# Moving the second group's loads, the last group's layer-norm statistics and the last projection steps in a one-core attention and gMLP block

## The chip, the cores and the metric

The kernel runs on one core of a Trainium2 chip. The core has five engines that run side by side and wait for each other on semaphores: TensorE (PE in the profile, with its weight loads as PEld), VectorE (DVE), ScalarE (ACT), GpSimd (POOL) and SyncE (SP), which here issues nearly all transfers. The metric is the device time of one execution in microseconds (us), taken as the median of several runs. A profiled execution is one further run; its span goes from the first to the last instruction.

## What is computed

One transformer block with adaptive layer norm: attention with a key and value cache, then a gMLP. Sizes: 2048 tokens of width 512, 32 query heads that share 8 key and value heads, head width 128, 2048 keys; in the MLP 896 columns in each half.

```python
sa, ca, ga, sb, cb, gb = split(silu(c) @ w_mod)          # six rows of 512
h = layernorm(x) * (1 + ca) + sa
x = x + ga * A(h)                                        # attention
h = layernorm(x) * (1 + cb) + sb
x = x + gb * B(h)                                        # gMLP

def A(x):
    q = (x @ wq).reshape(2048, 32, 128)                  # 4 query heads per kv head
    p = softmax(q @ k.T * 128 ** -0.5)
    return (p @ v).reshape(2048, 4096) @ wo

def B(x):
    z = gelu(x @ w_in)
    z1, z2 = z[:, :896], layernorm(z[:, 896:])
    g = w_sp @ z2 + b_sp[:, None]                        # w_sp is 2048 x 2048, over tokens
    return (z1 * g) @ w_out
```

## The kernel before

**Units and slots.** Attention is cut into 128 units: 8 groups g (one key and value head each, with its four query heads) of 16 units, one for each tile j of 128 tokens. Unit u belongs to group u // 16 and tile u % 16. Every unit is emitted in 8 slots. A slot of unit u has, in this order: what was put on a list for it (`at(unit, slot, function)`, L993), the two score products of unit u (`qk`, L1011 or L1030, into an `s_ps` bank pair) with the exponential that ACT takes of them (L1018 or L1037), the next share of the PV products of an earlier unit (`pv` L1086, `pv_rows` L1065, into an `o_ps` bank), a piece of a query projection for a later block (`fill`, L947, into a `misc` bank, copied out by DVE at L958), and in some slots one product of the output projection of a still earlier unit (`wo_proj`, L1143, into a `misc` bank). There are two `misc` banks, two `o_ps` banks and two pairs for `s_ps`. Each engine carries out its instructions in the order in which they are emitted; nothing reorders them.

**Units by rows.** From unit 8 up to 118 two of three units keep their probabilities by query rows, and four DMA transposes on SP for each such unit (L1050) turn them into the layout that PV needs. The other units compute the scores already turned and need none. The PV products of a unit run one to three units later, and the output projection two or three units after these. In units by rows each head has its own projection product, and DVE multiplies it by 1/sum while it adds it to `xacc` (L1136); in the others four products accumulate in one bank and DVE adds once (L1130). The output of a unit that is not by rows is turned by a DMA transpose (`oT`, L1109); in these units DVE takes a reciprocal (L1097) and a normalising multiply (L1098) of two heads at the end of slots 3 and 7.

**Loads of a group.** A group's wq, v, wo and k (512 KB each) are issued on SP by `load_wq` (L722), `load_v` (L730), `load_wo` (L740) and `load_k` (L745). From the third group on they go one at a time into units between units by rows. The first three of the second group go into unit 6, before the units by rows begin (L1296). In unit 5 POOL is given the rows `ga` and `gb`: it writes 2 KB of `mod` to memory (L1213) and reads it back spread over all partitions (L1214), once for each.

**Last group.** In the last group (units 112 to 127) the fourth projection product of a tile ends its attention. For tiles 0 to 11 POOL multiplies `xacc` by `ga` and adds `x` (L1159, L1160); for the last four tiles DVE does that. Then the layer-norm statistics follow at once on DVE (`ln_stats`, L698 and L699). `ln2` puts three steps on the list, counted from the unit in which the projection ended: `first` (POOL: 1/sqrt of the variance, L679 and L683) in the next unit's slot 0, `second` (DVE normalises, L687, and SP transposes, L1178) in its slot 4, `third` (DVE scales into `h2Ts`, L1185) one unit later in slot 5.

**The end.** The gMLP mixes tokens in four blocks of 512 tokens. The last block is done in two parts: 384 tokens, then the last 128 (tile 3 of the block). For these 128, each of seven column blocks f takes 16 products over the tokens (L1475), a product that adds the bias (L1495), and a DVE multiply with z1 into `yT` (L1503). One projection step (`o2_mm`, L1508) of the column block before stands between two blocks, as L1564 has it, and the seventh step closes the loop. Between the blocks `finish_tile` also ends the three other tiles (DVE L1520 and L1521, store on ACT's queue).

Of the kernel before, what the change touches and what calls it, by code (L numbers as in the profile page):

```python
# [575 lines left out]
def kernel(  # L576
# [28 lines left out]
    NT = S // P  # L605
    NDT = D // P
    NKT = SK // P
    NFT = FH // P
    NCH = S // 512
    CT = 512 // P  # L610
# [36 lines left out]
    x_sb = res.tile([P, NT, D], BF16, name="x_sb")  # L647
# [5 lines left out]
    mv2 = res.tile([P, NT, nc.vector.BN_AGGR_DIM], FP32, name="mv2")  # L653
# [16 lines left out]
    def bank(name):  # L670
        return psum.tile([P, 512], FP32, name=name)
# [4 lines left out]
    def rstd_of(mv, n, tag):  # L676

        ve = stat.tile([P, CT], FP32, name=f"ve_{tag}")
        nc.gpsimd.tensor_scalar(  # L679
            out=ve[:, :n], in0=mv[:, :, 1], scalar1=LN_EPS, scalar2=None, op0=ALU.add  # L680
        )
        rstd = stat.tile([P, CT], FP32, name=f"rstd_{tag}")
        nc.gpsimd.tensor_tensor(out=rstd[:, :n], in0=ve[:, :n], in1=mhalf[:, :n], op=ALU.pow)  # L683
        return rstd

    def normalise(dst, src, mv, rstd):
        nc.vector.tensor_scalar(  # L687
            out=dst,
            in0=src,
            scalar1=mv,  # L690
            scalar2=rstd,
            op0=ALU.subtract,
            op1=ALU.mult,
        )

    def ln_stats(mv, j, src):
        st = stat.tile([P, 1, nc.vector.BN_STATS_DIM], FP32, name="bnst")
        nc.vector.bn_stats(out=st[:, 0, :], in_=src)  # L698
        nc.vector.bn_aggr(out=mv[:, j, :], in_=st[:])  # L699
# [20 lines left out]
    def load_wq(g, engine):  # L720
        wqs[g] = early.tile([P, NDT, REP * DH], BF16, name="wq_g")
        engine.dma_start(  # L722
            out=wqs[g][:], in_=wq_dram[:, :, g * REP * DH : (g + 1) * REP * DH]
        )

    def load_v(g):
        v1 = late.tile([P, NKT, DV], BF16, name="v1")
        nc.gpsimd.memset(v1[:, :, DH:DV], 1.0)
        if g > 0:
            nc.sync.dma_start(out=v1[:, :, 0:DH], in_=v_dram[:, g])  # L730
        else:
            nc.sync.dma_start(out=v1[:, 0 : NKT // 2, 0:DH], in_=v_rows)
            nc.sync.dma_start(
                out=v1[:, NKT // 2 : NKT, 0:DH], in_=v_dram[:, 0, NKT // 2 : NKT]
            )
        groups.setdefault(g, {})["v1"] = v1

    def load_wo(g, engine):
        wo_g = late.tile([P, REP, D], BF16, name="wo_g")
        engine.dma_start(out=wo_g[:], in_=wo_dram[:, g * REP : (g + 1) * REP, :])  # L740
        groups[g]["wo"] = wo_g

    def load_k(g):
        kT = early.tile([P, SK], BF16, name="kT")
        nc.sync.dma_start_transpose(out=kT[:], in_=A_k_cache[0, g])  # L745
        groups.setdefault(g, {})["kT"] = kT
# [50 lines left out]
    def ln1_stats(j0, n):  # L797
        for j in range(j0, j0 + n):
            ln_stats(mv1, j, x_sb[:, j, :])
        return rstd_of(mv1[:, j0 : j0 + n, :], n, "ln1")  # L800
# [161 lines left out]
    first = dict(r1=ln1_stats(1, 1))  # L962
# [9 lines left out]
    def by_rows(u):  # L972
        return TURN_A <= u < TURN_B and (u - TURN_A) % len(LAGS) < len(LAGS) - 1
# [19 lines left out]
    def at(it, slot, fn):  # L993
        later.setdefault((it, slot), []).append(fn)
# [123 lines left out]
    def wo_proj(u):  # L1118
        g, j = divmod(u, NT)
        each = by_rows(u)  # L1120
        ps = {}

        def into(first, X_ps, scale):
            if first:
                xaccs[j] = late.tile([P, D], FP32, name=f"xacc{j}", bufs=1)
            xa = xaccs[j]
            if scale is None and first:
                nc.vector.tensor_copy(out=xa[:], in_=X_ps[:])
            elif scale is None:
                nc.vector.tensor_tensor(out=xa[:], in0=X_ps[:], in1=xa[:], op=ALU.add)  # L1130
            elif first:
                nc.vector.tensor_scalar(
                    out=xa[:], in0=X_ps[:], scalar1=scale, scalar2=None, op0=ALU.mult
                )
            else:
                nc.vector.scalar_tensor_tensor(  # L1136
                    out=xa[:], in0=X_ps[:], scalar=scale, in1=xa[:], op0=ALU.mult, op1=ALU.add
                )

        def mm(hh):  # L1140
            if hh == 0 or each:
                ps[0] = bank("misc")
            nc.tensor.matmul(  # L1143
                ps[0][:],
                lhsT=oTs[u][:, hh, :],
                rhs=groups[g]["wo"][:, hh, :],
                start=(hh == 0 or each),
                stop=(hh == REP - 1 or each),
            )
            if each:  # L1150
                c0 = u * REP + hh
                into(g == 0 and hh == 0, ps[0], rall[:, c0 : c0 + 1])
            elif hh == REP - 1:
                into(g == 0, ps[0], None)
            if hh < REP - 1 or g < HKV - 1:
                return
            xa = xaccs[j]
            engine = nc.gpsimd if j < NT - CT else nc.vector
            engine.tensor_tensor(out=xa[:], in0=xa[:], in1=ga_rows[:], op=ALU.mult)  # L1159
            engine.tensor_tensor(  # L1160
                out=x_sb[:, j, :], in0=xa[:], in1=x_sb[:, j, :], op=ALU.add
            )
            ln_stats(mv2, j, x_sb[:, j, :])

        return [lambda hh=hh: mm(hh) for hh in range(REP)]

    def ln2(it, j):

        st = {}

        def first():
            st["rstd"] = rstd_of(mv2[:, j : j + 1, :], 1, "ln2")

        def second():
            xn = res.tile([P, D], BF16, name="xn2", bufs=2)
            normalise(xn[:], x_sb[:, j, :], mv2[:, j, 0:1], st["rstd"][:, 0:1])
            st["xnT"] = res.tile([P, NDT, P], BF16, name="xnT2", bufs=2)
            nc.sync.dma_start_transpose(out=st["xnT"][:], in_=xn[:])  # L1178

        def third():  # L1180
            ch, c0 = j // CT, (j % CT) * P
            if ch not in h2Ts:
                h2Ts[ch] = res.tile([P, NDT, 512], BF16, name="hT", bufs=NCH)
            for dt in range(NDT):
                nc.vector.tensor_scalar(  # L1185
                    out=h2Ts[ch][:, dt, c0 : c0 + P],
                    in0=st["xnT"][:, dt, :],
                    scalar1=modc[:, 4 * NDT + dt : 4 * NDT + dt + 1],
                    scalar2=modc[:, 3 * NDT + dt : 3 * NDT + dt + 1],
                    op0=ALU.mult,  # L1190
                    op1=ALU.add,
                )

        at(it + 1, 0, first)
        at(it + 1, 4, second)
        at(it + 2, 5, third)

    def mod_cols_b():
# [86 lines left out]
    for g in range(1, HKV):  # L1285
        it = (g - 1) * NT
        loads = (
            (0, lambda g=g: load_wq(g, nc.sync)),
            (4, lambda g=g: load_v(g)),
            (6, lambda g=g: load_wo(g, nc.sync)),  # L1290
            (8, lambda g=g: load_k(g)),
        )
        last = it - 1
        for from_it, load in loads:
            if g == 1 and from_it < 8:
                at(6, 2, load)  # L1296
                continue
            last = next(u for u in pauses if u >= it + from_it and u > last)
            at(last + 1, 1, load)
# [93 lines left out]
    for it in range(NU + 6):  # L1393
# [26 lines left out]
        for u in wos:  # L1420
            if u >= (HKV - 1) * NT:
                ln2(it, u % NT)
# [84 lines left out]
    def o2_mm(dst, yT, jj, f):  # L1507
        nc.tensor.matmul(  # L1508
            dst,
            lhsT=yT[:, f, jj * P : (jj + 1) * P],  # L1510
            rhs=wout_sb[:, f, :],
            start=(f == 0),
            stop=(f == NFT - 1),
        )
# [34 lines left out]
    o2_last = [acc[jj // 2][:, (jj % 2) * 512 : (jj % 2 + 1) * 512] for jj in range(CT)]  # L1549
    yT = yTs[last]  # L1550
# [8 lines left out]
    for f in range(NFT):  # L1559
        spatial(last, yT, f, n_a, P, bias_by_pe=True)  # L1560
        if f == 0:
            for jj in range(CT - 1):
                o2_mm(o2_last[jj], yT, jj, NFT - 1)
        else:  # L1564
            o2_mm(o2_last[CT - 1], yT, CT - 1, f - 1)
        if f % 2 == 0 and f < 2 * (CT - 1):
            finish_tile(last, f // 2, o2_last[f // 2])
    o2_mm(o2_last[CT - 1], yT, CT - 1, NFT - 1)
    finish_tile(last, CT - 1, o2_last[CT - 1])
    fast.close()  # L1570

# [35 lines left out]
```

## Time and profile before

| what | us |
|---|---|
| median of 3 runs | 1313.06 (1312.56 to 1314.4) |
| profiled execution, whole | 1312.99 |
| its span, first to last instruction | 1311.2 |
| PE busy | 1300.0 |
| ACT busy | 1112.1 |
| DVE busy | 667.6 |
| POOL busy | 58.9 |
| granted clock of TensorE | 0.999 |

Times in views of the trace count from the start of the span. In a timeline the columns are the start, the duration, engine and line, the operation with output and inputs, the shape, how many instructions are merged, and in brackets how long the engine was idle before and whose result ended that. A product of 512 columns is listed with some 0.38 us, but the next one may start 0.215 us after it, since products are pipelined; the pitch, not the duration, tells what a product costs PE.

### The profile page before, as it was taken

Reading aid. Unit: us, or ns where it says so; the run is one execution under the profiler, and the core shown is the slowest. Engines: PE = TensorE matmul, PEld = TensorE weight load, DVE = VectorE, ACT = ScalarE, POOL = GpSimd, SP = SyncE. Lnnn points to the kernel's source line nnn. Section 1 sums busy time; section 2 is a strip of 40 time slices with the busy share of each in tenths; the row PEclk is TensorE's granted clock in tenths of the full one; section 3 lists DMA queues with packets and bytes.
Section 4 is the critical chain, followed back from the end, with each engine's and each line's share of the span. In section 5 each row is a group of like instructions: output and inputs, shape, how many; then the busy total and the mean of one; then the engine's idle time right before and its main releaser. Section 6 shows DMA issues by size and latency. Waiting matters only on the chain.

```text
span 1311.2 us, 22903 instructions
## 1 busy us (share of the span) xinstructions
PE 1300.0 (99%) x8807; PEld 705.3 (54%) x8807; DVE 667.6 (51%) x1730; ACT 1112.1 (85%) x1653; POOL 58.9 (4%) x96
## 2 busy tenths in 40 slices
PE   9999999999999999999999999999999999999998
PEld 5664555555555555555555555555555566644445
DVE  5633545444554455445545554555454565793443
ACT  7899999999999999999999999999999988650000
POOL 1100000000000000000000000000000134210000
PEclk9999999999999999999999999999999999999999
DMA  7499999999999999999999999999999821264300
GB/s 189 99 148 186 171 192 183 191 167 189 192 187 166 192 166 194 181 173 185 191 183 173 190 189 175 176 193 167 188 182 175 156 82 29 57 138 97 79 19 31
DMA packets 744102, 203.86 MB, mean 155 GB/s; under 512 B 728240, under 2 KB 742704, under 8 KB 743984
## 3 DMA queue, kind: packets, MB, share of 16 engines
q1 hardware_dynamic: 741168, 199.55, 83.6%
q10 hardware_dynamic: 2592, 2.23, 0.6%
q8 instruction: 71, 1.16, 0.4%
q0 software_dynamic: 224, 0.53, 0.2%
q14 instruction: 47, 0.39, 0.1%
HBM read 21.89 MB, written 2.10 MB: 18 GB/s over the span
## 4 chain that ended last, share of the span: by engine, by line
PE 98%; DVE 1%; DMA 0%; ACT 0%; POOL 0%; issue 0%; SPq 0%; ACTq 0%; DVEq 0%
PE s_ps L1011 20%; PE o_ps L1065 19%; PE o_ps L1086 15%; PE s_ps L1030 14%; PE misc L1143 8%; PE misc L947 8%; PE misc L1475 7%; PE s_ps L1310 2%; PE s_ps L1349 2%; PE o_ps L1508 1%; DMA wmod_a<-in_w_mod_dram 0%; PE s_ps L1508 0%; ACT win_sb L1018 0%; PE misc L857 0%; ACT pT L1037 0%; DVE hT L816 0%
## 5 line engine op out<-in xcount | busy, mean ns | idle before, releaser
L1037 ACT ACTIVATE pT<-s_ps 128x1024 bf16<-128x1024 f32 x408 | 413.2, 1025 | 33.6 <-PE s_ps L1030 15.6
L1011 PE MATMUL s_ps<-kT,qT 128*128 128x512 bf16 x1184 | 352.1, 379 | 0.0
L1018 ACT ACTIVATE win_sb<-s_ps 128x1024 bf16<-128x1024 f32 x298 | 304.6, 1023 | 3.2 <-ACT pn L1018 0.3
L1086 PEld LDWEIGHTS <-pT 128*128 128x128 bf16 x3264 | 218.5, 98 | 96.0 <-issue 0.2
L1030 PE MATMUL s_ps<-qT,kT 128*128 128x512 bf16 x864 | 256.7, 379 | 1.3 <-ACT pT L1037 1.2
L1086 PE MATMUL o_ps<-v,pT 128*128 128x129 bf16 x3264 | 251.6, 220 | 0.0
L1136 DVE SCALAR_TENSOR_TENSOR xacc<-misc,rall,xacc 128x512 f32<-128x512 f32 x290 | 216.9, 748 | 54.8 <-PE misc L1143 48.5
L1018 ACT ACTIVATE pn<-s_ps 128x1024 bf16<-128x1024 f32 x196 | 200.5, 1023 | 1.7 <-PE s_ps L1011 0.4
L1143 PE MATMUL misc<-wo_g,oT 128*128 128x512 bf16 x512 | 194.0, 379 | 2.7 <-DVE xacc L1136 2.7
L1065 PEld LDWEIGHTS <-v 128*128 128x128 bf16 x1184 | 115.8, 98 | 139.8 <-issue 0.4
L947 PE MATMUL misc<-hT,wq_g 128*128 128x512 bf16 (+2 forms) x520 | 187.0, 371 | 0.1
L1065 PE MATMUL o_ps<-wsp,v 128*128 128x512 bf16 x592 | 176.1, 379 | 0.0
L1065 PE MATMUL o_ps<-pT,v 128*128 128x512 bf16 x592 | 175.4, 379 | 0.0
L1011 PEld LDWEIGHTS <-qT 128*128 128x128 bf16 x1184 | 115.7, 98 | 104.8 <-issue 1.2
L958 DVE CAST qT<-misc 128x512 bf16<-128x512 f32 x125 | 85.7, 686 | 153.0 <-PE misc L947 153.0
L1030 PEld LDWEIGHTS <-kT 128*128 128x128 bf16 x864 | 83.4, 98 | 90.4 <-issue 6.6
L1054 DVE TENSOR_TENSOR tot<-rs 128x1 f32<-128x1 f32 x296 | 45.2, 153 | 166.1 <-ACT win_sb L1018 112.0
L1475 PE MATMUL misc<-wsp,z 128*128 128x512 bf16 (+2 forms) x560 | 100.7, 336 | 0.0
L1018 ACT ACTIVATE wmod_a<-s_ps 128x1024 bf16<-128x1024 f32 x98 | 100.3, 1024 | 0.0
L1475 PEld LDWEIGHTS <-z 128*128 128x128 bf16 x560 | 50.6, 98 | 48.7 <-issue 0.2
L1097 DVE RECIPROCAL rall<-o_ps 128x2 f32<-128x2 f32 x108 | 18.0, 167 | 111.0 <-PE o_ps L1086 110.9
L947 PEld LDWEIGHTS <-wq_g 128*128 128x128 bf16 x528 | 50.4, 98 | 37.3 <-issue 0.4
(105 smaller groups left out, 791.4 us busy)
## 6 DMA issues: line engine op xcount, KB each, us to landing
wo_g<-in_A_wo_dram SPq DMA_DIRECT2D x8, 512.0 KB, 5.0
wq_g<-in_A_wq_dram SPq DMA_DIRECT2D x7, 512.0 KB, 4.5
v<-in_A_v_cache_dram SPq DMA_DIRECT2D x7, 512.0 KB, 4.7
wsp<-in_w_mod_dram SPq DMA_DIRECT2D x1, 2048.0 KB, 8.5
out_dram<-yout ACTq DMA_DIRECT2D x16, 128.0 KB, 1.7
win_sb<-in_B_w_in_dram SPq DMA_DIRECT2D x1, 1792.0 KB, 7.1
x_sb<-in_A_x_dram SPq DMA_DIRECT2D x3, 512.0 KB, 4.9
wsp<-win_sb SPq DMA_TRANSPOSE x75, 4.7
```

Of the source, the lines that this page charges most:

```text
L947: nc.tensor.matmul(ps[0][:, o0 : o0 + n], lhsT=wqs[g][:, dt, hh * DH : (hh + 1) * DH], rhs=hTs[ch][:, dt, c0 : c0 + n], start=(dt == 0), s ...
L958: nc.vector.tensor_copy(out=dst, in_=src)
L1011: nc.tensor.matmul(s_ps[:, c * 512 : (c + 1) * 512], lhsT=qTs[b][:, hh, jj * P : (jj + 1) * P], rhs=groups[g]["kT"][:, k0 : k0 + 512], sta ...
L1018: nc.scalar.activation(out=rows_of(u, hh)[:, half * HK : (half + 1) * HK], in_=s_ps[:], func=ACT.Exp, scale=inv_sqrt_dh, accum_out=rsums[u ...
L1030: nc.tensor.matmul(s_ps[:, h * 512 : (h + 1) * 512].rearrange("p (r q) -> p r q", r=REP), lhsT=groups[g]["kT"][:, kt * P : (kt + 1) * P], ...
L1037: nc.scalar.activation(out=pTs[u][:, 2 * i : 2 * i + 2, :], in_=s_ps[:].rearrange("p (k q) -> p k q", k=2), func=ACT.Exp, scale=inv_sqrt_dh,)
L1054: nc.vector.tensor_tensor(out=tot[:], in0=rs[:, 2 * hh : 2 * hh + 1], in1=rs[:, 2 * hh + 1 : 2 * hh + 2], op=ALU.add)
L1065: nc.tensor.matmul(o_pss[u][:], lhsT=groups[g]["v1"][:, kt, 0:DH], rhs=pTs[u][:, kt, :], start=(kt == 0), stop=(kt == NKT - 1),)
L1086: nc.tensor.matmul(o_ps[:, hh % 2, 0 : DH + 1], lhsT=pTs[u][:, kt, hh * P : (hh + 1) * P], rhs=groups[g]["v1"][:, kt, 0 : DH + 1], start=( ...
L1136: nc.vector.scalar_tensor_tensor(out=xa[:], in0=X_ps[:], scalar=scale, in1=xa[:], op0=ALU.mult, op1=ALU.add)
L1143: nc.tensor.matmul(ps[0][:], lhsT=oTs[u][:, hh, :], rhs=groups[g]["wo"][:, hh, :], start=(hh == 0 or each), stop=(hh == REP - 1 or each),)
L1475: nc.tensor.matmul(g_pss[f][:, :n], lhsT=z2[:, st, f * P : (f + 1) * P], rhs=wsp[t][:, st, c0 : c0 + n], start=(st == 0), stop=(st == NT - ...
```

## The change

Three edits, all of them to where instructions stand.

1. The first three loads of the second group are put into three different slots: wq in unit 6 slot 2 as before, v in unit 7 slot 2, wo in unit 7 slot 5. They stay in this order on SP; one output transpose (`oT`) now stands between wq and v instead of after wo.
2. For tiles 0 to 11 of the last group the statistics leave `wo_proj` and become the start of `first`, which moves from slot 0 to slot 3 of the next unit; `second` moves from slot 4 to slot 5. The last four tiles stay as they were.
3. In the last part of the last block, the projection steps of column blocks 0, 1 and 2 stay between the blocks, and steps 3 to 6 follow after the seventh block.

```diff
@@ in wo_proj
             engine.tensor_tensor(
                 out=x_sb[:, j, :], in0=xa[:], in1=x_sb[:, j, :], op=ALU.add
             )
-            ln_stats(mv2, j, x_sb[:, j, :])
+            if j >= NT - CT:
+                ln_stats(mv2, j, x_sb[:, j, :])
@@ in ln2
         def first():
+            if j < NT - CT:
+                ln_stats(mv2, j, x_sb[:, j, :])
             st["rstd"] = rstd_of(mv2[:, j : j + 1, :], 1, "ln2")
...
-        at(it + 1, 0, first)
-        at(it + 1, 4, second)
+        at(it + 1, 0 if j >= NT - CT else 3, first)
+        at(it + 1, 4 if j >= NT - CT else 5, second)
         at(it + 2, 5, third)
@@ loads
             if g == 1 and from_it < 8:
-                at(6, 2, load)
+                at(6 + from_it // 4, 2 + 3 * (from_it // 2 % 2), load)
                 continue
@@ the last 128 tokens
         if f == 0:
             for jj in range(CT - 1):
                 o2_mm(o2_last[jj], yT, jj, NFT - 1)
-        else:
+        elif f < CT:
             o2_mm(o2_last[CT - 1], yT, CT - 1, f - 1)
         if f % 2 == 0 and f < 2 * (CT - 1):
             finish_tile(last, f // 2, o2_last[f // 2])
-    o2_mm(o2_last[CT - 1], yT, CT - 1, NFT - 1)
+    for f in range(CT - 1, NFT):
+        o2_mm(o2_last[CT - 1], yT, CT - 1, f)
     finish_tile(last, CT - 1, o2_last[CT - 1])
```

## The prediction

> **What bounds the kernel now.** I read the page's busy times first, then the waits, then timelines around each gap of PE. The page:
>
> ```profile
> span 1311.2 us, 22903 instructions
> PE 1300.0 (99%) x8807; PEld 705.3 (54%) x8807; DVE 667.6 (51%) x1730; ACT 1112.1 (85%) x1653; POOL 58.9 (4%) x96
> ```
>
> PE is busy in 99% of the span and the granted clock is 0.999, so only PE's gaps can be won. Between 123.5 and 1028 us the table of windows has PE busy 904.50 of 904.50 us. What remains is the start, the tail after PE's last product, and a few gaps. The waits of PE, and one of DVE:
>
> ```profile
> PE misc L1143 <- DVE xacc L1136: 2.7, 1, 2.7
> PE s_ps L1030 <- ACT pT L1037: 1.2, 2, 0.9
> PE s_ps L1508 <- DVE yT L1503: 0.2, 1, 0.2
> DVE bnst L698 <- POOL x_sb L1160: 31.4, 12, 2.6
> ```
>
> The columns after the colon are total us, times and the longest. Each of the first three lies where one edit works. Second group's loads, in unit 6 (slots start at 64.96 and every 1.10 us):
>
> ```profile
> 67.28 0.58 SPq L722 DMA_DIRECT2D wq_g<-in_A_wq_dram  x1
> 68.45 6.93 SPq L740 DMA_DIRECT2D wo_g<-in_A_wo_dram  x1
> 71.58 3.89 ACT L1037 ACTIVATE pT<-s_ps 128x1024 bf16<-128x1024 f32 x4 [1.66 <-PE s_ps L1030]
> 72.65 0.59 PE L1030 MATMUL s_ps<-qT,kT 128*128 128x512 bf16 x2 [0.93 <-ACT pT L1037]
> ```
>
> ACT starts at 71.58 on a product that PE ended at 69.95 (the pair at 69.36 plus 0.59): nothing computed was late. PE's next pair starts at 72.65 instead of 70.46 + 1.10 = 71.56, so PE loses 1.09. SP meanwhile sits 6.93 us in issuing wo.
>
> Last group, unit 123:
>
> ```profile
> 1086.09 1.15 POOL L1160 TENSOR_TENSOR x_sb<-xacc,x_sb 128x512 bf16<-128x512 f32 x1
> 1087.28 0.69 DVE L698 BATCH_NORM_STATS2 bnst<-x_sb 128x6 f32<-128x512 bf16 x1 [2.61 <-POOL x_sb L1160]
> 1088.11 0.72 DVE L1136 SCALAR_TENSOR_TENSOR xacc<-misc,rall,xacc 128x512 f32<-128x512 f32 x1
> 1088.88 0.38 PE L1143 MATMUL misc<-wo_g,oT 128*128 128x512 bf16 x1 [2.68 <-DVE xacc L1136]
> 1092.77 0.38 PE L1143 MATMUL misc<-wo_g,oT 128*128 128x512 bf16 x1
> ```
>
> DVE works in order: it waits for Pool's two sums, the multiply-add that empties a `misc` bank stands behind, and PE waits for the bank. The product at 1088.88 would have followed the one before it at 1086.04 (1085.82 plus the pitch of 0.215), so 2.84 are lost. Eleven more such DVE waits cost PE 0.12 together (a PV product at 1121.64). The end:
>
> ```profile
> 1304.96 0.38 PE L1508 MATMUL s_ps<-wout_sb,yT 128*128 128x512 bf16 x1
> 1305.16 0.29 DVE L1503 TENSOR_TENSOR yT<-misc,z1T 128x128 bf16<-128x128 f32 x1 [0.76 <-PE misc L1495]
> 1305.51 0.39 PE L1508 MATMUL s_ps<-wout_sb,yT 128*128 128x512 bf16 x1 [0.17 <-DVE yT L1503]
> 1305.94 0.69 DVE L1520 TENSOR_TENSOR tmp<-s_ps,gb_rows 128x512 bf16<-128x512 f32 x1 [0.48 <-PE s_ps L1508]
> ```
>
> The last product could follow 0.215 after the one before it (the pitch of 512 columns), at 1305.18; it waits for the last yT.
>
> **The change, part by part.** No arithmetic is added or removed; each edit moves instructions.
>
> *Last projection steps.* The spatial blocks f = 4, 5, 6 lose the projection step between them (three of 0.215); these three and the last one follow at the end. Blocks 5 and 6 start 0.215 and 0.43 earlier, so the bias product of block 6 starts at 1304.91 - 0.43 = 1304.48 and the last yT ends at 1305.45 - 0.43 = 1305.02. The three held steps run from 1304.54 to 1305.18 and cover that multiply; the last product starts at 1305.18 instead of 1305.51. DVE's yT of block 5 still begins behind the output sum of tile 2 (1303.77 + 0.42), before it is needed at 1304.97. Gain 0.33. If the three did not run beside that multiply, the last product would come at 1305.08 + 0.645 = 1305.73, a loss of 0.22: bounds -0.33 to +0.22.
>
> *Statistics half a unit later.* Twelve pairs (0.69 + 0.18) move from behind the sums to slot 3 of the next unit, with Pool's two small rstd steps (0.22 + 0.57); the normalisation and its transpose on SP move from slot 4 to 5. Pool's sums take 1.27 + 1.15, so they are over before slot 3 except where two tiles end in one unit (tile 7 in unit 124, tile 10 in 126). There the second pair waits for Pool 1 to 1.6 us in front of a reciprocal and onorm (0.17 + 0.42) whose PSUM bank is wanted only four slots (3.5 us) later. Rstd is ready 1.95 after a pair starts (1087.28 to 1089.15 plus a signal), two slots are 1.8 to 2.6, so a wait of the normalisation stays within a few tenths, and only onorm and multiply-adds of later slots stand behind it. On SP the transpose lets one transpose of unit 117 pass; it is used eight slots later.
> Unit 123 by hand: first multiply-add at 1085.14 to 1085.88, so slot 1's product starts at 1086.04 unhindered; slot 2 at 1087.36; its multiply-add to 1088.52. Then the statistics of tile 6 run, 1088.44 to 1089.35, in the busiest slot: reciprocal 1089.27, onorm 1089.44, the qT copy 1089.78 to 1090.46. Slot 4's product would start at 1089.77 and needs the bank that this copy empties: 0.74 late, where now it is 0.16 late (1092.77 against 1092.61). So of 2.84 + 0.12, 0.58 comes back: gain 2.38. Bounds: 2.96 if nothing comes back, 1.6 if the wait in slot 4 also covers the next multiply-add (to 1091.12, 0.66 more).
>
> *Second group's loads.* v and wo leave slot 2 of unit 6 for unit 7; in SP's order an output transpose (of unit 5) now stands between wq and v. That transpose waits for onorm, ready at about 74.4, so SP holds v and wo until about 75.5 whatever the slot says. SP is no longer pushing three loads at once in 68 to 75. If that is what froze ACT's start, PE gains 1.09. But everything behind matters too. Transposes of the row units fill SP from 85.33 on:
>
> ```profile
> 85.33 8.13 SPq L1050 DMA_TRANSPOSE wsp<-win_sb  x3
> 115.95 5.46 SPq L1050 DMA_TRANSPOSE wsp<-pn  x2
> 124.02 0.59 PE L1065 MATMUL o_ps<-wsp,v 128*128 128x512 bf16 x2
> ```
>
> They are issued back to back up to 133.81, the DMA share of 74.85 to 123.5 is full, and the last of unit 11's four lands at 123.9 by the trace's landing events, while PE wants it at 123.96. So PE's gain is kept only if this chain also starts earlier (ACT's earlier finish allows 84.24), and any delay of it beyond that is paid in full at 124. Bounds of this edit: -1.09 to +5.4 (below). I take 1.09, as PE's lost time and SP's long issue coincide, and v and wo have from 75.5 to 84 to land (v took 4.7 us on median).
>
> Sum against the profiled execution: 1312.99 (span 1311.2 and 1.8 around it) - 0.33 - 2.38 - 1.09 = 1309.19. That execution lies 0.07 under the median 1313.06: 1309.3.
>
> **Rivals.**
> *The freeze isn't the loads'.* The list of transfers for 60 to 80 us speaks for it:
>
> ```profile
> hT<-xn SPq DMA_TRANSPOSE x4, 9.0
> mod<-modc POOLq DMA_DIRECT2D x2, 2.0 KB, 11.7
> ```
>
> Pool's 2 KB writes of `mod` (issued 60.10, waited for until 71.99) take 11.7, and four transposes issued before any load land after 9.0, where over the whole run that kind takes 2.9. Then the freeze stays and the edit is worth nothing; or PE's gain is handed back at 124. Only 2.71 remain: 1310.3. Against it: in the second such write (72.56 to 84.3) ACT does not stall, and SP is not issuing then.
> [...]
>
> *Row transposes late (the slower side).* v and wo now move during the second mod write. In the same stretch wo took 16.6 to land. If both have to wait for its end at 84.9, 1 MB at 191 GB/s, the rate of the row slices, is 5.5 us in front of unit 8's transposes; unit 11's land at 129.4, PE stalls there for 5.4 and what it had gained. The whole is then 1313.06 - 2.71 + 5.4 = 1315.7. It decides from 2.7 us of lateness on; less gives 1310.4 to 1313. For: the landing just in time. Against: v lands before the freeze in the present run, and Pool's ga rows, no longer behind v, may end the second write sooner.
>
> *DVE held by Pool.* DVE's first multiply-add of unit 123 would now run beside Pool's sums, which it never does today. If Pool's two sums held it until 1087.24, slot 1's product would start 2.1 us late, and only 0.9 of the 2.96 would be won: 1311.1 with the loads' gain. Against: Pool's small steps at 1088.28 left the multiply-add at 0.72, like the others (0.74).
> [...]
>
> **How the numbers follow.** All three gains: 0.38, at 1309.3 (1308.4 to 1310.0 by the bounds). Loads worth nothing: 0.27, 1310.3 (1309.9 to 1311.0). Row transposes a little late: 0.14, 1310.4 to 1313. Late enough to be slower: 0.13, about 1315.7. DVE held: 0.08, 1311.1. The range 1308.4 to 1313.2 leaves out the slower case and a little below. A measurement of this kernel can tell about 0.2%, 2.6 us: faster means under 1310.4, the first case and some 0.6 of the second, 0.54; slower means over 1315.7, most of the late case, 0.11; within, 0.35.
>
> **What would show it.** DVE's wait for Pool at L698 nearly gone, PE's 2.7 at L1143 gone and a wait of about 0.7 some 4 us later; the last projection products at an even pitch of 0.215; no ACT start 1.6 late near 70; PE's first product of unit 13 without a wait. Wrong would be a PE wait for wsp near 123, an ACT stall of the old size, or a multiply-add on DVE that starts only after Pool's sums.

## The result and the profile after

| | us | against before in the same comparison |
|---|---|---|
| before, median of 11 runs | 1314.40 (1312.56 to 1315.09) | |
| changed kernel, median of 11 runs | 1311.13 (1310.30 to 1312.87) | 0.9979, interval 0.9969 to 0.9988 |
| profiled execution of the changed kernel | 1312.48, span 1310.7 | 1312.99 before |

The median fell by 3.3 us (0.25%); by the ratio, which the means of the eleven runs give too, the kernel became 0.21% faster. The two profiled executions differ by 0.5 only: that of before was among the shortest of its kernel, that of the changed kernel among the longest. So the median can't be read off these two traces; they show which waits came and went. The busy times of the changed kernel, then the waits of PE and the wait of DVE for Pool (total us, times, the longest):

```profile
span 1310.7 us, 22899 instructions
PE 1299.7 (99%) x8807; PEld 705.4 (54%) x8807; DVE 672.8 (51%) x1730; ACT 1112.7 (85%) x1653; POOL 59.6 (5%) x96
```

```profile
DVE bnst L698 <- POOL x_sb L1160: 19.3, 8, 2.6
PE o_ps L1065 <- DVE rall L1057: 1.8, 2, 0.9
PE s_ps L1030 <- ACT pT L1037: 1.6, 2, 1.3
PE misc L1143 <- DVE qT L958: 0.6, 1, 0.6
```

PE's 2.7 for `xacc` at L1143 and its 0.2 for the last `yT` are gone. In their place stand 0.6 for the qT copy, and two waits at L1065 that before did not have. The wait for ACT has grown from 1.2 to 1.6. DVE still waits for Pool eight times. By stage, first the statistics, unit 123 (timeline):

```profile
1086.81 1.27 POOL L1159 TENSOR_TENSOR xacc<-xacc,ga_rows 128x512 f32<-128x512 f32 x1 [3.92 <-DVE xacc L1130]
1087.20 0.75 DVE L1136 SCALAR_TENSOR_TENSOR xacc<-misc,rall,xacc 128x512 f32<-128x512 f32 x1 [0.47 <-PE misc L1143]
1090.50 0.68 DVE L698 BATCH_NORM_STATS2 bnst<-x_sb 128x6 f32<-128x512 bf16 x1
1091.83 0.68 DVE L958 CAST qT<-misc 128x512 bf16<-128x512 f32 x1
1092.56 0.38 PE L1143 MATMUL misc<-wo_g,oT 128*128 128x512 bf16 x1 [0.57 <-DVE qT L958]
```

This trace runs 2.06 us late against that of before here: Pool's multiply starts at 1086.81, before at 1084.75. DVE's first multiply-add now runs at 1087.20, beside that multiply, at its usual length (0.75). The statistics start 3.69 us after Pool's multiply does, where it was 2.53, and so ahead of the qT copy, and one product starts at 1092.56 instead of 1091.83 (eight PV products start at 1091.38 and take 0.45): the gap is 0.73.

The end:

```profile
1304.20 0.22 PE L1498 MATMUL misc<-bsp_bc,mean_bf 128*128 128x128 bf16 x1
1304.26 1.03 PE L1511 MATMUL s_ps<-wout_sb,yT 128*128 128x512 bf16 x4
1304.46 0.29 DVE L1506 TENSOR_TENSOR yT<-misc,z1T 128x128 bf16<-128x128 f32 x1 [0.35 <-PE misc L1498]
```

Four products of 0.215 pitch in 1.03 us (3 x 0.215 and the length of the last, 0.38): no gap before the last one, the last `yT` (to 1304.75) is done during the three held steps.

The loads. Here nothing went as wanted:

```profile
66.99 0.58 SPq L722 DMA_DIRECT2D wq_g<-in_A_wq_dram  x1
71.90 1.94 ACT L1037 ACTIVATE pT<-s_ps 128x1024 bf16<-128x1024 f32 x2 [2.07 <-PE s_ps L1030]
72.98 0.59 PE L1030 MATMUL s_ps<-qT,kT 128*128 128x512 bf16 x2 [1.34 <-ACT pT L1037]
...
76.01 0.81 SPq L730 DMA_DIRECT2D v<-in_A_v_cache_dram  x1
76.88 4.07 SPq L740 DMA_DIRECT2D wo_g<-in_A_wo_dram  x1
...
100.88 0.59 PE L1065 MATMUL o_ps<-wsp,v 128*128 128x512 bf16 x2 [0.94 <-DVE rall L1057]
126.07 0.59 PE L1065 MATMUL o_ps<-wsp,v 128*128 128x512 bf16 x2 [0.86 <-DVE rall L1057]
```

ACT's late start is there with only wq on its way (2.07 idle, before 1.66); PE's gap is 1.50 instead of 1.09. PE then waits at 100.88 (gap 1.10) and 126.07 (gap 1.02, before 0.05). The view names DVE's `rall`, but the operand `wsp` is what came last: by the trace's landing events unit 8's fourth transpose has landed at 100.7 (before at 98.5) and unit 11's at 125.9 (before at 123.9). wo, issued at 76.88, has landed at 89.04; before it had at 85.05.

### The profile page after: what moved, and what is told of

It reads as the page before. It is cut to its first block, busy times and chain, and to the rows that moved or that the text cites. A ratio compares the mean times of both kernels' runs of the same rounds, so it can differ in the third digit from the quotient of the medians.

```text
span 1310.7 us, 22899 instructions
## 1 busy us (share of the span) xinstructions
PE 1299.7 (99%) x8807; PEld 705.4 (54%) x8807; DVE 672.8 (51%) x1730; ACT 1112.7 (85%) x1653; POOL 59.6 (5%) x96
## 3 DMA queue, kind: packets, MB, share of 16 engines
q10 hardware_dynamic: 2592, 2.23, 0.6%
## 4 chain that ended last, share of the span: by engine, by line
PE 98%; ACT 1%; DVE 1%; DMA 0%; issue 0%; SPq 0%; ACTq 0%; DVEq 0%
PE s_ps L1011 20%; PE o_ps L1065 19%; PE o_ps L1086 15%; PE s_ps L1030 14%; PE misc L1143 8%; PE misc L947 8%; PE misc L1478 7%; PE s_ps L1313 2%; PE s_ps L1352 2%; PE o_ps L1511 1%; PE s_ps L1511 0%; DMA wmod_a<-in_w_mod_dram 0%; ACT pT L1037 0%; ACT win_sb L1018 0%; PE misc L857 0%; ACT wmod_a L1018 0%
## 5 line engine op out<-in xcount | busy, mean ns | idle before, releaser
L1143 PE MATMUL misc<-wo_g,oT 128*128 128x512 bf16 x512 | 194.0, 379 | 0.6 <-DVE qT L958 0.6
L1065 PEld LDWEIGHTS <-v 128*128 128x128 bf16 x1184 | 115.7, 98 | 141.9 <-issue 2.7
L1065 PE MATMUL o_ps<-wsp,v 128*128 128x512 bf16 x592 | 176.1, 379 | 1.8 <-DVE rall L1057 1.8
L1065 PE MATMUL o_ps<-pT,v 128*128 128x512 bf16 x592 | 175.4, 379 | 0.0
```

The costliest lines, as they stand in the source:

```text
L1065: nc.tensor.matmul(o_pss[u][:], lhsT=groups[g]["v1"][:, kt, 0:DH], rhs=pTs[u][:, kt, :], start=(kt == 0), stop=(kt == NKT - 1),)
L1143: nc.tensor.matmul(ps[0][:], lhsT=oTs[u][:, hh, :], rhs=groups[g]["wo"][:, hh, :], start=(hh == 0 or each), stop=(hh == REP - 1 or each),)
```

## The experiments

All are compared with before in runs of the same chip. Medians of before in the three sets: 1314.46 (e1 to e4), 1314.11 (e5 to e8), 1314.78 (e9 to e12). Each set ran on a chip of its own, so between sets only the distances from before can be compared, and these within some tenths. A gap of PE is the start of a product minus the start of the one before it minus its pitch.

**Which edit did it.** e1 is edits 2 and 3 (the loads put back), e2, e3 and e4 are the edits 1, 2 and 3 one at a time.

```diff
# e1: the changed kernel with
-                at(6 + from_it // 4, 2 + 3 * (from_it // 2 % 2), load)
+                at(6, 2, load)
```

> Edits 2 and 3 without the moved loads. Theory A (the loads are not what freezes ACT near 70 us; Pool's 2 KB writes of mod are): the freeze stays at 1.1 to 1.5 us of PE, the time is 2.7 us under before (ratio 0.9979) and not above the changed kernel. Theory B (moving the loads gains on average, and the profiled run of the changed kernel was an unlucky one): 1 us slower than the changed kernel, 1.7 under before (ratio 0.9987).

> Only the moved loads. Theory A: between no change and 2.5 us slower than before (ratio 1.000 to 1.002), with ACT's late start near 71.6 still there and PE waiting for turned probabilities in units 10 and 13. Theory B: 1.1 us faster (ratio 0.9992).

> Only the later statistics. Worked out by hand: PE's wait of 2.8 us in unit 123 gone, a wait of 0.7 in its slot 4 in place of 0.16, so 2.4 us under before (ratio 0.9982). If VectorE were held by Pool's sums: a wait of about 2.1 us in slot 1 of unit 123 and 0.9 us gained at most (ratio 0.9993).

> Only the held projection steps. From the last bias product (L1495) to the last projection product: 0.70 us instead of 0.60, but that bias product 0.43 earlier, so the end 0.33 us earlier (ratio 0.99975, not to be told from 1 by the time; the trace decides by the pitch of the last four products, 0.215 without a wait). If the held steps are not covered: 0.2 us later.

| | median (lowest to highest) | ratio to before | PE's gap near 72, near 1089 |
|---|---|---|---|
| e1, edits 2 and 3 | 1310.26 (1309.15 to 1310.40) | 0.9967, 0.9955 to 0.9979 | 0.51, 0.74 |
| e2, loads | 1314.73 (1313.78 to 1316.43) | 1.0004, 0.9995 to 1.0013 | 0.95, 2.84 |
| e3, statistics | 1310.64 (1310.13 to 1311.22) | 0.9974, 0.9963 to 0.9985 | 1.07, 0.73 |
| e4, end | 1314.15 (1312.08 to 1315.18) | 0.9997, 0.9988 to 1.0007 | 1.00, 2.85 |

The statistics bring everything that the medians can show. The end is worth 0.3 in the trace, too little for the medians. The loads bring nothing: ACT's late start is there with them (e2) as without them (e1), and in e2 the transposes of unit 11 come late for PE:

```profile
PE o_ps L1065 <- DMA wsp<-pn: 0.5, 1, 0.5
```

The changed kernel is 3.3 below its before and e1 4.2 below its own, so the loads seem to cost 0.9; e2 says 0.3. The intervals of the changed kernel and e1 overlap, and e2's holds 1, so by the medians a cost of the loads is not shown; a gain of 1.09 (ratio 0.9992) lies outside e2's interval. The runs of the changed kernel spread over 2.6 us, e1's over 1.3.

Not all of this was expected: e1 and e3 are 4.2 and 3.8 below before instead of 2.7 and 2.4, e1's gap near 72 is 0.51 and not 1.1 to 1.5, and of e2's waits in units 10 and 13 only the second came. The surplus of e1 and e3 is taken up further down.

**What freezes ACT.** Pool's two writes of `mod` move 2 KB each, by the kernel's layout (L1213) in 512 pieces of 4 bytes. e5 and e6 leave them out and set the two rows to 0.01, so that their output is another one.

```diff
# e5: edits 2 and 3, and; e6: all three edits, and
-            line = dram.tile([D], FP32, name=f"mod{part}")
-            nc.gpsimd.dma_start(out=line[:].rearrange("(dt p) -> p dt", p=P), in_=modc[:, cols])
-            nc.gpsimd.dma_start(out=rows[:], in_=line[:].partition_broadcast(P))
+            nc.gpsimd.memset(rows[:], 0.01)
```

> Edits 2 and 3 alone, as in e1, and Pool's transfers of mod are left out: neither the two writes of 512 values of 4 bytes each nor the two broadcasts that read them back are made, and the rows ga and gb are set to 0.01 by a memset, so the output is another one. Theory (the late start of ACT near 72 us comes from the 4-byte writes of mod): no late start remains, so the gap of PE near 72 us (0.51 in e1's profiled run, 0.95 to 1.50 in the others) is below 0.1, and the time is 0.5 to 1.1 us below e1's, about 1309.4. Rival (it is the three loads of 512 KB after all): the gap stays at 0.5 to 1.1 us and the time at 1310.3. Where the gap stays and an hT transpose or wq ends it, it is neither.

> All three edits, and Pool's transfers of mod left out as in e5. Theory: edit 1 as such does no harm near 72 us, so the gap there is below 0.1; v and wo still land late, so what is left of edit 1's cost are unit 8's transposes: PE waits near 101 and 126 us of together 0 to 2 us. If the late transposes of unit 8 come from where v and wo stand on SP, these waits stay at 1 us each and the time is 1 to 2 us above e5's; if they came from the 4-byte writes, which held back v and wo in turn, they vanish and the time equals e5's within 0.3.

e5: 1308.96 (1308.83 to 1309.26), e6: 1308.83 (1308.69 to 1309.42). In both PE's products follow at their pitch near 72 us, the late start of ACT is gone, and no product waits at 101 or 126. With the writes away the edited loads cost nothing, and gain nothing. e5 lies 5.15 below its before and e1 4.20 below its own: 0.95 between them, as expected (0.5 to 1.1). The four hT transposes, 9.1 in the changed kernel, land after 2.4 in e5 (transfers issued from 60 to 80 us; the last figure is the median time to landing):

```profile
hT<-xn SPq DMA_TRANSPOSE x4, 2.4
```

e5 and e6 took the writes and the broadcasts that read them back away together. e8 and e12 tell these two apart: the broadcasts stay, and only the writes take another form.

**The writes in larger pieces, and the statistics one slot later.** In e7 the wait that was given back in unit 123 is attacked; e8 is e7 with the rows turned on PE, so that each write has four pieces of 512 bytes; e12 is the changed kernel with these pieces.

```diff
# e7: edits 2 and 3, and
-        at(it + 1, 0 if j >= NT - CT else 3, first)
-        at(it + 1, 4 if j >= NT - CT else 5, second)
+        at(it + 1, 0 if j >= NT - CT else 4, first)
+        at(it + 1, 4 if j >= NT - CT else 6, second)
# e8: e7, and; e12: all three edits, and
+        modb = res.tile([P, 2 * NDT], BF16, name="modb")
+        nc.vector.tensor_copy(out=modb[:], in_=mc_ps[:, 0 : 2 * NDT])
+        def turned():
+            t_ps = bank("misc")[:].bitcast(BF16)
+            nc.tensor.transpose(t_ps[0 : 2 * NDT, 0:P], modb[:], ident[:])
+            modr = res.tile([2 * NDT, P], FP32, name="modr")
+            nc.vector.tensor_copy(out=modr[:], in_=t_ps[0 : 2 * NDT, 0:P])
...
-            nc.gpsimd.dma_start(out=line[:].rearrange("(dt p) -> p dt", p=P), in_=modc[:, cols])
+                nc.gpsimd.dma_start(
+                    out=line[:].rearrange("(dt p) -> dt p", p=P),
+                    in_=modr[i * NDT : (i + 1) * NDT, :],
+                )
...
+        at(5, 5, turned)
```

> Edits 2 and 3 with the moved steps one slot later: the statistics of tiles 0 to 11 at slot 4 of the next unit and the normalisation at slot 6, the loads as before. Theory (the 0.58 given back in unit 123 is the statistics standing in front of the copy of qT in the one slot in which DVE has both): the wait of PE for that copy, 0.73 in all runs with edit 2, is at most 0.2, no multiply-add comes late instead, and the time is 0.3 to 0.6 below e1's. Rival (DVE is as full in slot 4): a wait of 0.3 to 0.8 moves to the product of slot 5, near 1091 us, and the time equals e1's.

> As e7, and mod's two rows are turned on PE first (as bf16, one product of 128 columns in unit 5) and then written to memory as eight pieces of 512 bytes instead of 1024 pieces of 4 bytes; the broadcasts that read them back stay. Theory (the many small writes hold the queue): the gap of PE near 72 us is below 0.1, the added product and copy cost at most 0.1 to 0.3, and the time is 0.3 to 0.9 below e7's; this would be the fastest version. Rival (the reads back, 256 KB each, or the loads): the gap stays at 0.5 to 1.1 and the time equals e7's or lies 0.1 to 0.3 above it.

> All three edits, and mod's two rows written as eight pieces of 512 bytes as in e8. Theory (the 4-byte writes are what made edit 1 cost time): no gap of PE near 72, 101 or 126 us, the wait of 0.73 in unit 123 stays, and the time is e8's plus 0.58 within 0.3, about 1309.2, which is 1.9 below the changed kernel. Rival (edit 1's place on SP is late by itself): waits of PE near 101 or 126 us of 0.3 to 1.0 each, and a time of 1309.6 to 1311.

e7: 1309.75 (1309.64 to 1309.95). The gap for the qT copy falls from 0.73 to 0.16 and no later product waits; DVE's wait for Pool in front of the statistics (L698) is gone in all tiles, while its waits for `rstd` (L687, 5.0 in 7 times) stay. e8: 1308.67 (1308.42 to 1309.04), ratio 0.9961 (0.9947 to 0.9975): the fastest version, 5.4 below before and 1.1 below e7, where 0.3 to 0.9 was expected. Its gap near 72 is gone; the added product and what stands around it cost PE two gaps of 0.09 to 0.10 at 60 us. The transfers of e8 in that stretch:

```profile
hT<-xn SPq DMA_TRANSPOSE x4, 3.4
mod<-modr POOLq DMA_DIRECT2D x2, 2.0 KB, 2.8
```

The same 2 KB land after 2.8 instead of 11.3 in the changed kernel, and the transposes beside them after 3.4 instead of 9.1, with the broadcasts still made (e7, from which only the form of the writes and the turn ahead of them set e8 apart, has 11.5 and 9.5). So it is the form of the writes that freezes ACT and holds back the transposes. e12: 1309.49 (1309.45 to 1309.86), no gap near 72, 101 or 126, and the 0.73 in unit 123, as expected. It spreads over 0.4 us; the changed kernel, which differs only in these writes and the turn ahead of them, over 2.6.

**Why the statistics bring more than the gap.** 2.84 + 0.12 - 0.57 is 2.39; e3 is 3.8 below before. In e2's profiled execution PE's stall is followed by something that before's does not have. The same stretch after the stall, first in before, then in e2 (busy times with instructions in brackets for PE, PEld, DVE, ACT, POOL; then the granted clock, DMA share, GB/s):

```profile
1089.00:1092.50 3.50, 3.50 (x34) 2.22 (x33) 2.47 (x5) 2.19 (x3) 0.15 (x1) 1.00 0.00 0
```

```profile
1089.00:1092.50 3.50, 3.50 (x19) 2.04 (x19) 1.50 (x2) 1.14 (x2) 0.23 (x1) 0.59 0.00 0
```

PE is called busy in both, yet it started 34 products in one and 19 in the other, at a granted clock of 0.59. From 1089.68 to 1092.90 they follow each other at twice their pitch; the excess, added up from their starts, is 1.62 us. The traces of before and e4, whose stalls are 2.84 and 2.85 long, do not show this. Three kernels test whether the length of the stall decides it.

```diff
# e9: before, and of edit 2 only tile 6 (statistics at slot 3, normalisation at slot 5)
-            ln_stats(mv2, j, x_sb[:, j, :])
+            if j != 6:
+                ln_stats(mv2, j, x_sb[:, j, :])
# e10: before, and ahead of Pool's sum
+            if j == 6:
+                again = res.tile([P, P], FP32, name="again")
+                for i in range(3):
+                    part = slice(i * P, (i + 1) * P)
+                    nc.gpsimd.tensor_tensor(
+                        out=again[:], in0=xa[:, part], in1=ga_rows[:, part], op=ALU.mult
+                    )
# e11: before, and
-            engine.tensor_tensor(out=xa[:], in0=xa[:], in1=ga_rows[:], op=ALU.mult)
+            scale = nc.vector if j == 6 else engine
+            scale.tensor_tensor(out=xa[:], in0=xa[:], in1=ga_rows[:], op=ALU.mult)
```

> Of edit 2 only tile 6 (the one whose statistics stall PE in unit 123): its statistics at slot 3 of unit 124's list and its normalisation at slot 5; the other eleven tiles, the loads and the end as before. What is in question: edit 2 gained 3.8 us by the medians (e3) but 2.4 to 3.0 by the gaps in the trace. Theory (the 2.84 stall is followed, in most executions, by some 3 us in which PE's products come at half pace, as in the profiled run of e2 from 1089.68 to 1092.90 with a granted clock of 0.59 and 1.62 us lost): tile 6 alone brings nearly all of it, the median is 1310.3 to 1311.0, 3.4 to 4.1 below before, the mean granted clock of every run is 0.999 or 1.000, and the runs lie within 1.5 us. Rival (the other tiles' waits on Pool cost the rest): the median is 1311.5 to 1312.2, and some runs show 0.998.

> Before, with three further multiplies of 128 columns on Pool for tile 6 (their result is not used) between its multiply by ga and its sum, so that PE's stall near 1088 us grows from 2.84 by about 1.0 to 1.2 us. Theory (after a stall of this length the clock drops): now every execution has the half pace, so all runs show 0.998 or less, none lies at before's lower cluster plus 1.1 (about 1313.9), and the median is that of before's runs with 0.998 plus the stall, 1315.5 to 1316.3. Rival (the drop of the clock has nothing to do with the stall's length): the runs split into two clusters as before's do, both 1.1 higher.

> Before, with DVE instead of Pool for tile 6's multiply by ga; Pool's sum stays. The stall near 1088 us should shrink from 2.84 to about 2.2 to 2.4. Theory: the drop of the clock comes less often or never, so the runs gather at 1312.0 to 1312.8 with a granted clock of 0.999, and the median is 1.5 to 2.3 below before's although the stall is only about 0.5 shorter. Rival (the length does not matter): the same share of runs at 0.998, and the median 0.5 below before's.

| | PE's gap in unit 123 | median (lowest to highest) | runs with a mean clock of 0.998 or less |
|---|---|---|---|
| before, all three sets | 2.84 | 1314.11 to 1314.78 | 41 of 61 |
| e9 | 0.73 | 1311.29 (1310.92 to 1312.61) | 0 of 9 |
| e11 | 2.23 | 1314.18 (1312.65 to 1315.72) | 6 of 11 |
| e10 | 4.32 | 1317.25 (1315.77 to 1318.68) | 11 of 11 |

Before's 41 runs with the lower clock have a median of 1314.89, its 20 others 1313.08: a difference of 1.8, near the 1.62 that e2's trace shows. The 59 runs of the kernels without the stall (changed, e1, e3, e5 to e9, e12) all have a mean clock of 0.999 or 1.000. e9, one tile of twelve, brings 3.5 of e3's 3.8; its median is above the 1311.0 expected at most, its distance from before as expected. In e10 the stall is 1.48 longer (1.0 to 1.2 was expected) and the median 2.5 higher, above the 1315.5 to 1316.3 expected, and no run kept the full clock. Its trace has the clock falling while PE still stands, and staying low for the products behind it:

```profile
1087.00:1089.50 2.50, 0.00 (x0) 0.00 (x0) 0.08 (x1) 0.26 (x1) 2.23 (x4) 0.95 0.00 0
1089.50:1091.00 1.50, 0.00 (x0) 0.00 (x0) 1.43 (x3) 0.00 (x0) 0.50 (x2) 0.50 0.00 0
1091.00:1095.50 4.50, 4.48 (x22) 2.56 (x22) 1.50 (x2) 1.46 (x2) 0.29 (x1) 0.50 0.00 0
```

e11's expectation missed: 0.61 off the stall did not make the drop rarer (6 of 11; before in the same set has 13 of 25), and the median fell by 0.6 only. Its profiled execution has the half pace too (1.35 us, from 1089.80 to 1092.49). The stretches at half the clock, whole, in e2, e11 and e10:

```profile
1089.63:1093.05 3.42, 3.42 (x21) 2.32 (x21) 1.25 (x2) 1.69 (x2) 0.00 (x0) 0.50 0.00 0
1089.74:1093.15 3.41, 3.19 (x19) 2.04 (x18) 1.25 (x4) 1.94 (x2) 0.00 (x0) 0.50 0.00 0
1089.27:1096.09 6.82, 4.88 (x23) 2.90 (x24) 3.17 (x6) 2.05 (x2) 0.90 (x3) 0.50 0.00 0
```

On both sides of each the clock is 1.00. e10's is twice as long as the others, and its products lose some 2.2 us by the same count as in e2: the 1313.08 of before's other runs with 1.48 and 2.2 make 1316.8, near the 1317.25 measured.

Gaps of 0.73 were followed by it in no trace, and neither were the gaps near 72 us of 1.50 in the changed kernel, 1.60 in e11 and 2.19 in e10. So from 2.2 to 2.85 it happens in some executions and not in others; what decides in a single one stays open. The mean clock is given to three places, and 1.62 us are 0.0012 of the time, so the last column sorts the runs only roughly.

## Why the prediction was right or wrong

*The end: right.* 0.33 off, as worked out.

*The statistics: the gap right to 0.01, the gain too small.* The product of slot 4 was forecast 0.74 late and is 0.73 late; DVE's multiply-add beside Pool's sums keeps its 0.75, so the rival "DVE held by Pool" falls. Two things were not seen. First, the term of 2.38 counts only the time in which PE stands; in two thirds of before's executions, by their mean clock, the products behind the stall run at half pace, and the moved statistics end that too (1.6 to 1.8 more). Before's one profiled execution did not have it, and with 0.999 its mean clock looked faultless: the sum was made against the lucky third of a spread that the three given times already hinted at (1312.56 to 1314.4). Second, the sentence that Pool's sums are over before slot 3 but for tiles 7 and 10 is wrong: DVE still waits eight times, six of them 2.6 as before and two 1.8. None of these costs PE anything, as before; e9 shows that tile 6 was what mattered.
In the traces that have it the granted clock is 0.50, for 3.42 us in e2, 3.41 in e11 and 6.82 in e10; by the mean clock it came in 41 of 61 runs of before. PE had been idle for 2.68 us (e2) and 2.06 us (e11) ahead of it; before's profiled execution, idle for 2.68 too, does not have it. So an idle time of two microseconds was not safe here, and one of 2.68 not always harmful.

*The loads: wrong.* The step that failed is "I take 1.09, as PE's lost time and SP's long issue coincide". They do coincide, but e5 and e8 show the cause beside them, the 4-byte writes that Pool had issued 10 us earlier: take them away or give them 512-byte pieces, and three loads at once freeze nothing. This is the first rival, with its hT transposes that land after 9; its counter-argument (ACT does not stall in the second write) weighed too much. The second rival, row transposes late, came true as well in its mild form: v and wo moved into the second write, wo landed 4.0 later, and PE paid 1.10 at 101 and 0.97 at 126 (1.02 less the 0.05 of before). So the term measured +0.41 + 1.10 + 0.97 = +2.5 in the profiled execution, and between +0.3 (e2) and +0.9 (changed kernel and e1) by the medians, where -1.09 stood.
Landings waited beside the writes although SP had issued them and Pool the writes: SP's four hT transposes took 9.1 us in the changed kernel, 2.4 without the writes (e5) and 3.4 beside writes of 512-byte pieces (e8). The writes themselves took 11.3 in 4-byte pieces (changed kernel) and 2.8 in 512-byte pieces (e8); no run here tries sizes between.

*The sum.* The forecast gain was 3.8, the measured one 3.3. It came out near by luck, because two errors of opposite sign met: some 1.6 to 1.8 too little for the statistics, 1.09 and a further 0.3 to 0.9 too much for the loads. Statistics 2.39 + 1.6 and end 0.33 make 4.3, near e1's 4.2; loads of -0.3 to -0.9 leave 3.4 to 4.0. The time itself, forecast at 1309.3, came out at 1311.13, 1.8 higher: 1.3 of that is before's own median, 1313.06 in the three runs that the sum started from and 1314.40 in eleven.

## What to carry to other kernels

Price a stall of the bottleneck engine by what follows it too: look at the granted clock in the stretch behind every gap of two microseconds or more (here it was 0.50 behind gaps of 2.23 in e11 and 2.84 in e2), and in more than one execution. When an engine starts late although its operand was long done (ACT 1.6 us in before), look for a transfer of tiny pieces (4 bytes here) in flight ahead of everything else, and not only for the largest transfer; landing times far above the usual ones for the same kind (9.0 instead of 2.9 in before) give it away. And an edit that only spaces transfers moves them into the next stretch (wo landed 4.0 us later in the changed kernel): check what is in flight there.

## What the runs showed of the hardware

- A write of 2 KB in 4-byte pieces held back the landing of transposes from 2.4 (e5) to 9.1 us (changed kernel) and the start of an ACT instruction whose operand PE had ended 1.0 (e1) to 2.7 us (e10) before. PE's gap from it differs between profiled executions (0.51, 0.90, 0.95, 1.00, 1.07, 1.09, 1.13, 1.50, 1.60, 2.19) and is absent in all four kernels without such writes (e5, e6, e8, e12). How a transfer delays a signal between PE and ACT, no run shows.
- After PE had stood 2.1 to 2.7 us in unit 123, its clock fell to one half for 3.41 to 3.42 us in two of four profiled executions (e2 and e11, not before and e4) and, by the mean clock, in 6 of 11 runs (e11) and 41 of 61 (before); in a stand of 4.2 us (e10) it fell 2.4 us in, for 6.82 us in the one profiled, and by the mean clock in all 11 runs.
- Pool's sums beside DVE's multiply-adds from PSUM slowed neither in unit 123 (1.27 and 0.75 together in the changed kernel, 1.27 and 0.75 apart in before).
